# Attention with decay and a mixture of experts on one core: the recorded order of the steps, written anew

## The chip, the cores and the metric

The kernel runs on one core of a Trainium2 chip. The metric is the device time of one execution in microseconds (us). The core's engines are TensorE (PE in the profile, its weight loads PEld), VectorE (DVE), ScalarE (ACT), GpSimd (POOL) and SyncE (SP), which issues nearly all transfers; each works off its own instructions in order and waits for the others at semaphores.

## The reference

Eight batches of eight attention heads (576 positions, 64 columns) with a decay of the scores, then a layer of four experts, each an attention of its own on the 512 columns that the heads give together.

```python
scores = scale * np.matmul(q, k.transpose(0, 1, 3, 2))
cum = np.cumsum(np.log(np.clip(f, 0.0001, 1.0)), axis=-1)
scores = np.where(causal, -1e9, scores + cum[:, :, :, None] - cum[:, :, None, :])
attn = np.exp(scores - np.max(scores, axis=-1, keepdims=True))
attn_out = np.matmul(attn / (np.sum(attn, axis=-1, keepdims=True) + 1e-09), v)
x = attn_out.transpose(0, 2, 1, 3).reshape(B, S, H * D)
for e in range(E):
    q, k, v = x @ wq[e], x @ wk[e], x @ wv[e]
    a = softmax(causal(scale * (q @ k.transpose(0, 2, 1))))
    out += top_two_weight[e] * (a @ v @ wo[e])
```

## The kernel before

The work comes in units of two heads (or two experts): a0_0 to a7_3 are pair 0 to 3 of batch 0 to 7, m0_0 to m7_1 the two pairs of experts of a batch. A name in a profile row is cut to its kind, so ka_a there is the tile ka of some attention unit, ka_m that of a unit of experts; in the listings of the order it keeps its unit, as ka_a1_1.

An attention unit goes through these stages:

- **prep_attn** loads both heads' q and k as xin (L390), and splits them into a high part, rounded by ScalarE's copies (L393, L396), and a low part, the difference of the two, which the subtraction at L406 makes. There are two of it per unit, one per half of the partitions, each 64 partitions by 1152 columns with both inputs in SBUF. VectorE does them, except the first of the units 1 to 3, which GpSimd does. The second subtraction's output ka is what the second half of each scores matmul (L726) reads.
- **max_pass** finds the largest score of each block of rows: matmuls of the high parts into PSUM banks m0 to m3 (L625), VectorE's reductions of them (L631 and L647, inputs in PSUM; L680 and L687 for the last 64 rows) into the tile mxs, a transpose by TensorE (L692), and a copy by ScalarE (L695) that goes back into kq by a transfer. GpSimd first fills a corner of mxs (L621, 64 x 2). The first unit has a form of its own (L585 to L610).
- **scores** computes the scores in banks s0 to s3, two matmuls a piece (L726, L727); ScalarE's exponentials take them into P (L744, L756, L762, L779, L784), GpSimd sets what lies above the diagonal to zero (L713, L747, L786).
- **row_sums**: GpSimd adds up the pieces of P that belong to the same rows in the tile R, for each head one sum of 128x448 (L792), one of 128x320 (L794) and one of 128x192 (L796), and a last one of 64x128 for both (L798). The second and third add to what the one before it wrote in the same half of R. The tile is of 128 partitions, and all their inputs are in SBUF.
- **attend** (L817) multiplies P by the values, **apply_rows** divides by the sums (L855 on TensorE, L870, L873, L875, L884 on VectorE with ScalarE's fill L881 between them, a transfer L890, the product L902).

The experts' units begin with projections (L551 on TensorE, L559 and L564 behind it), and then take the same way.

Every stage of every unit is a Python generator that stops after each step. The table ORDER, two digits in base 64 per step, 5323 steps, says which generator is to go on next, and at the end each engine's instructions are bound to the order in which they were recorded:

```python
for x, y in zip(digits[::2], digits[1::2]):
    i = DIGITS.index(x) * len(DIGITS) + DIGITS.index(y)
    if i not in started:
        started[i] = iter(tasks[i]())
    next(started[i], None)
```

So the table is the order of the work on every engine and in every queue. A second table, SLOTS, says for each kind of tile which buffer the next tile takes, in the order in which they are asked for. The kernel opens with 110 small matmuls that do no work of the reference (L212), spread among the first steps.

Of the kernel before, what the change touches and what calls it, by code (L numbers as in the profile page):

```python
# [27 lines left out]
4w4w4w4w4w4w4w4w4w4w4w4w4w4w4w4w4w4w4w4w4w4w4w4w4w4w4w4w4w4w4w4w4w4w4w4w4w4w4w4w4w4w4w4w4w4w4w4w4w4x4x4x4x000500  # L28
4y4y004x4x4y024y4y4A4y4y4y4y004w4A4w4A4A4w4w4w4A4A4A014A4A4A4A054w4w4w4w4w4w4w050505054w4w4w4w4w4w024w4w4w4w4w4w
4w4w4w4w4w4w4w4w4w0000000000024w024w0202020202020202020c4z4w4w4w4w4w4z074w07074w0207020202020202020202024A4w4w4w  # L30
4w05020202020202050c060c4w4w4w4w07074w4w4A4w020202054w4w0c0c034y0c4y030307070c4w4w4w070703034A4A0703030303070707
030707030303030303074y0h0e4z0707070303030303030303030303034z0707070707074z0e0e0e070e4z0707074z4z0e0e0e0e0e040c0e
0e0e0e0e0e0e0e0j0e0h0h0h0c0h0e0e08080h0e0e03080e0808080h08080808080808080808080o08080t0A0e030j0j0j0j0j0j0j080808
03084w4w0e0e040e0j0j0j0808080o0808030j0j0j0j0j0j0j0j0j0j084w080j0j0j0j0j090e0v0e0o090j0q0t0h0j0o0f0o0f0o0o0j0j0f
0f0f0f0f0f0f030f0f0f0f0f0f0f0f0f0q0q0q0q0q0q0k0q080f0f0q0q0q0f0d080f0f0k0f0f0i080t0f0t030q080k0k0k0k0k0q0q0q0q0q
# [1024 lines left out]
```

## Time and profile before

| | |
|---|---|
| time, median of three runs | 658.17 us (656.69 to 658.58) |
| the profiled execution | 657.54 us |
| its span in the trace | 655.5 us |
| TensorE busy | 633.0 us, 97% |
| VectorE busy | 564.6 us, 86% |
| ScalarE busy | 480.9 us, 73% |
| GpSimd busy | 469.9 us, 72% |
| transfers | 76.91 MB, 117 GB/s |

A row of a timeline has the start of an instruction in us, its duration, its engine and line, the operation, output and inputs, their shapes, how many of them follow each other, and in brackets how long the engine had sat idle before it and what ended that. An instruction that has been taken up by its engine and is held up inside it shows as a long one, without idle time. A windows row has, for a stretch of the span, its length, the busy time of each engine with the number of instructions, the granted clock of TensorE (1.00 is 2.4 GHz, 0.50 is 1.2 GHz), and what the DMA engines did.

### The profile page before, as it was taken

The numbers are of one execution on the slowest core, as the hardware profiler recorded it, in microseconds if no ns is written. First come the engines' busy times: TensorE is split into PE (matmuls) and PEld (weight loads), VectorE is DVE, ScalarE is ACT, GpSimd is POOL, SyncE is SP. The second block draws the span as 40 slices with busy tenths as digits, with TensorE's granted clock in tenths as the row PEclk, the third lists the DMA queues.
The fourth block names the chain that finished last, engine by engine and source line by source line (L and its number), as shares of the span: only waits on it lengthen the run. The fifth ranks groups of instructions, "written<-read, shape, count | busy, mean of one in ns | idle before, by whom it ended". The sixth has DMA issues, their size and how long they took to land.

```text
span 655.5 us, 15384 instructions
## 1 busy us (share of the span) xinstructions
PE 633.0 (97%) x5303; PEld 542.0 (83%) x5303; DVE 564.6 (86%) x1541; ACT 480.9 (73%) x1057; POOL 469.9 (72%) x759
## 2 busy tenths in 40 slices
PE   8897989999999999999999999999999999999997
PEld 6674778888978789779887888977988788979976
DVE  6889798998899998988989899898888998877672
ACT  7896578696777967788677875787758887665644
POOL 9998487879677795769838874877577968814850
PEclk9999899999999999999999999999999999999999
DMA  5553342633454443454544523716344622421236
GB/s 188 156 180 95 91 135 76 180 103 100 95 122 125 135 116 122 123 134 102 148 129 83 142 79 80 196 34 192 95 127 112 197 64 76 110 60 39 61 78 212
DMA packets 33532, 76.91 MB, mean 117 GB/s; under 512 B 4395, under 2 KB 4875, under 8 KB 33455
## 3 DMA queue, kind: packets, MB, share of 16 engines
q1 hardware_dynamic: 33455, 75.94, 42.7%
q8 instruction: 42, 0.69, 0.4%
q14 instruction: 35, 0.29, 0.1%
HBM read 32.86 MB, written 10.35 MB: 66 GB/s over the span
## 4 chain that ended last, share of the span: by engine, by line
PE 76%; DVE 10%; ACT 4%; POOL 4%; DMA 3%; issue 2%; SPq 0%; POOLq 0%; DVEq 0%; ACTq 0%
PE pp_m L551 14%; PE ob_a L817 7%; PE s_a L726 6%; PE po L952 6%; PE s_a L727 6%; PE pv L446 6%; PE m_a L625 6%; PE ob_m L817 4%; PE m_m L625 4%; PE s_m L727 3%; PE s_m L726 3%; DVE ka_a L406 3%; PE oa_a L817 3%; PE sm_a L855 2%; DVE junk_a L631 2%
## 5 line engine op out<-in xcount | busy, mean ns | idle before, releaser
L726 PE MATMUL s_a<-ka_a 128*128 128x320 f32 (+4 forms) x384 | 105.7, 301 | 2.4 <-DVE ka_a L406 1.2
L727 PE MATMUL s_a<-kq 128*128 128x320 f32 (+4 forms) x384 | 103.4, 297 | 0.7 <-DMA kq<-ms_a 0.7
L631 DVE CUSTOM_DVE_ANT_0 junk_a<-m_a,mask 128x192 bf16<-128x192 f32 (+2 forms) x186 | 86.6, 484 | 7.7 <-PE m_a L625 5.2
L625 PE MATMUL m_a<-kq 128*128 128x448 f32 (+3 forms) x372 | 78.1, 305 | 7.2 <-DVE mxs_a L631 6.2
L559 ACT ACTIVATE kq<-pp_m 64x288 fp32r<-64x288 f32 x128 | 51.7, 404 | 34.5 <-PE pp_m L551 32.7
L792 POOL TENSOR_TENSOR R_a<-P_a 128x448 f32<-128x448 f32 x64 | 74.6, 1166 | 0.0
L726 PEld LDWEIGHTS s_a<-ka_a 128*128 128x128 f32 (+1 forms) x384 | 70.3, 183 | 4.9 <-ACT kq L559 1.4
L713 POOL TENSOR_SCALAR_AFFINE_SELECT P_a<-P_a 128x128 f32<-128x128 f32 x128 | 51.2, 408 | 29.5 <-ACT P_a L779 14.2
L747 POOL TENSOR_SCALAR_AFFINE_SELECT P_a<-P_a 128x256 f32<-128x256 f32 x64 | 37.8, 599 | 47.9 <-ACT P_a L744 47.3
L727 PEld LDWEIGHTS s_a<-kq 128*128 128x128 f32 (+1 forms) x384 | 69.7, 183 | 2.2 <-DMA kq<-ms_a 0.9
L564 DVE TENSOR_TENSOR ka_m<-pp_m,kq 64x288 fp32r<-64x288 f32 x128 | 58.2, 455 | 13.1 <-ACT kq L559 9.8
L625 PEld LDWEIGHTS m_a<-kq 128*128 128x128 f32 x372 | 58.5, 182 | 12.8 <-DVE mxs_a L631 7.9
L817 PE MATMUL ob_a<-P_a,va 128*64 128x320 f32 (+1 forms) x512 | 67.6, 406 | 0.0
L794 POOL TENSOR_TENSOR R_a<-R_a,P_a 128x320 f32<-128x320 f32 x64 | 63.8, 997 | 3.3
L406 DVE TENSOR_TENSOR ka_a<-xin_a,ka_a 64x1152 fp32r<-64x1152 f32 x32 | 58.3, 1821 | 0.8
L817 PEld LDWEIGHTS ob_a<-P_a,va 128*64 128x64 f32 x512 | 36.0, 137 | 23.8
L726 PE MATMUL s_m<-ka_m 128*128 128x256 f32 (+3 forms) x192 | 51.4, 294 | 0.0
L727 PE MATMUL s_m<-kq 128*128 128x256 f32 (+3 forms) x192 | 50.8, 293 | 0.0
L631 DVE CUSTOM_DVE_ANT_0 junk_m<-m_m,mask 128x448 bf16<-128x448 f32 (+2 forms) x96 | 44.6, 486 | 6.4 <-PE m_m L625 5.5
L744 ACT ACTIVATE P_a<-s_a 128x512 f32<-128x512 f32 x64 | 36.6, 593 | 13.1 <-PE s_a L727 12.4
L796 POOL TENSOR_TENSOR R_a<-R_a,P_a 128x192 f32<-128x192 f32 x64 | 43.1, 674 | 2.8
L406 DVE TENSOR_TENSOR ka_a<-xin_a,kq 64x1152 fp32r<-64x1152 f32 x29 | 41.5, 1431 | 2.7 <-PE s_m L726 1.9
(206 smaller groups left out, 2096.3 us busy)
## 6 DMA issues: line engine op xcount, KB each, us to landing
xin_a<-in_qk_dram SPq DMA_DIRECT2D x32, 576.0 KB
va<-in_v_dram SPq DMA_DIRECT2D x32, 320.0 KB
bt_a<-rr_a SPq DMA_DIRECT2D x32, 288.0 KB
ka_m<-kq SPq DMA_DIRECT2D x32, 288.0 KB
kq<-ka_a SPq DMA_DIRECT2D x30, 288.0 KB
out_dram<-outb SPq DMA_DIRECT2D x32, 256.0 KB
bt_m<-rr_m SPq DMA_DIRECT2D x16, 288.0 KB
kq<-ex SPq DMA_DIRECT2D x45, 27.0 KB
```

The source lines that it names most:

```text
L406: eng.tensor_tensor(lo, x[at], hi.bitcast(F32), ALU.subtract)
L551: nc.tensor.matmul(pp[:, :HS], w[:, c, es], x[c][:, gs], start=(n == 0), stop=(n == 3 * KC - 1))
L559: nc.scalar.activation(hv[h], src[h], AF.Copy)
L564: nc.vector.tensor_tensor(lo[:, h, gs], src[h], hv[h].bitcast(F32), ALU.subtract)
L625: nc.tensor.matmul(dst, qB[0:K, h, i0 : i0 + dst.shape[0]], kB[0:K, h, j0:j1], start=True, stop=True)
L631: nc.vector.tensor_tensor_reduce(jk[:, :n], src, mask[:, MW - n :], 1.0, init, ALU.add, ALU.max, acc)
L713: return nc.gpsimd.affine_select(pv, pv, [[1, 128]], ALU.is_ge, 0.0, base=0, channel_multiplier=-1)
L726: nc.tensor.matmul(dst, kaf[:, c : c + m], qA[:, h, i0:i1], start=True, stop=False)
L727: nc.tensor.matmul(dst, kqf[0:K, c + h * S : c + h * S + m], qB[0:K, h, i0:i1], start=False, stop=True)
L792: g.tensor_tensor(r[:, h, 128:S], q[:, 320:768], q[:, 768:1216], ALU.add)
L794: g.tensor_tensor(r[:, h, 256:S], r[:, h, 256:S], q[:, 1216:1536], ALU.add)
L817: mm = nc.tensor.matmul(dst[64 * h : 64 * h + 64, c0 : c0 + rhs.shape[-1]], vs[h][0:kp, blk], rhs, start=first, stop=last,)
```

## The change

The tables ORDER and SLOTS are replaced; no other line differs, so line numbers are the same in both kernels, as are the number and the shapes of the instructions of every engine. ScalarE's fill of the reciprocals (L881) stays what it was. Of SLOTS the lines P, wide, banks, mxs, strips and mxt differ.

```diff
 ORDER = """
-4w4w4w4w4w4w4w4w4w4w4w4w4w4w4w4w4w4w4w4w4w4w4w4w4w4w4w4w4w4w4w4w4w4w4w4w4w4w4w4w4w4w4w4w4w4w4w4w4w4x4x4x4x000500
+4w4w4w4w4w4w4w4w4w4y4y4y4y4y4y4y4y4y4w4x4x4x4x000005024w4w4w4w4w4w4w4w4w4w4w4w4w4w4w4w004x004A064w4w4w4w4w4w4w4w
...
 SLOTS = """
-mxs 010101101011001010110101101011010110100101010101
+mxs 010010001011001010110010100011010111010101010101
```

What that moves is shown at three places.

**First, the start, on VectorE.** The first unit's reductions of its first head end with L604; then the kernel before has one of the second unit's reductions (a0_1), and after it the second head of the first unit.

```order
L602 TENSOR_TENSOR mx0_a0_0_282<-m2_a0_0_277,mask_83 64x64
L604 TENSOR_REDUCE mxs_a0_0_182<-mx0_a0_0_282 64x1
L631 ISA junk_a0_1_301,mxs_a0_1_293<-m0_a0_1_296,mask_83 128x192
L631 ISA mxs_a0_1_293 128x1
L595 ISA junk_a0_0_310,mxs_a0_0_182<-m1_a0_0_308,mask_83 128x192
```

```order
L602 TENSOR_TENSOR mx0_a0_0_288<-m2_a0_0_279,mask_83 64x64
L604 TENSOR_REDUCE mxs_a0_0_148<-mx0_a0_0_288 64x1
L595 ISA junk_a0_0_310,mxs_a0_0_148<-m1_a0_0_308,mask_83 128x192
L595 ISA mxs_a0_0_148 128x1
L599 TENSOR_REDUCE mxt_a0_0_217<-m0_a0_0_312 128x1
```

The reduction of a0_1 now stands behind the whole of the second head and behind the subtraction L406 of a0_1.

**Second, the row sums of a0_2 and a0_3 on GpSimd, and VectorE beside them.** GpSimd in the kernel before, from the last zeroing of a0_3 on, and then in the changed one.

```order
L786 AFFINE_SELECT pl0_91<-pl0_91 64x128
L796 TENSOR_TENSOR R_a0_2_725<-R_a0_2_725,P_a0_2_698 128x192
L792 TENSOR_TENSOR R_a0_2_725<-P_a0_2_698 128x448
L792 TENSOR_TENSOR R_a0_3_853<-P_a0_3_775 128x448
L794 TENSOR_TENSOR R_a0_2_725<-R_a0_2_725,P_a0_2_698 128x320
L794 TENSOR_TENSOR R_a0_3_853<-R_a0_3_853,P_a0_3_775 128x320
L796 TENSOR_TENSOR R_a0_2_725<-R_a0_2_725,P_a0_2_698 128x192
L796 TENSOR_TENSOR R_a0_3_853<-R_a0_3_853,P_a0_3_775 128x192
L792 TENSOR_TENSOR R_a0_3_853<-P_a0_3_775 128x448
L621 MEMSET mxs_a1_2_973 64x2
L794 TENSOR_TENSOR R_a0_3_853<-R_a0_3_853,P_a0_3_775 128x320
```

```order
L796 TENSOR_TENSOR R_a0_2_724<-R_a0_2_724,P_a0_2_662 128x192
L786 AFFINE_SELECT pl0_91<-pl0_91 64x128
L792 TENSOR_TENSOR R_a0_3_842<-P_a0_3_772 128x448
L621 MEMSET mxs_a1_1_872 64x2
L794 TENSOR_TENSOR R_a0_3_842<-R_a0_3_842,P_a0_3_772 128x320
L792 TENSOR_TENSOR R_a0_2_724<-P_a0_2_662 128x448
L796 TENSOR_TENSOR R_a0_3_842<-R_a0_3_842,P_a0_3_772 128x192
L792 TENSOR_TENSOR R_a0_3_842<-P_a0_3_772 128x448
L794 TENSOR_TENSOR R_a0_2_724<-R_a0_2_724,P_a0_2_662 128x320
L794 TENSOR_TENSOR R_a0_3_842<-R_a0_3_842,P_a0_3_772 128x320
L796 TENSOR_TENSOR R_a0_2_724<-R_a0_2_724,P_a0_2_662 128x192
L796 TENSOR_TENSOR R_a0_3_842<-R_a0_3_842,P_a0_3_772 128x192
```

Both tables interleave the sums of the two units. In the kernel before a fill of 64 x 2 (L621) stands behind eight sums; in the changed one it stands behind two, ahead of eight.

On VectorE at the same time stands the subtraction L406 of ka_a1_1 that is the second of its unit, first in the kernel before.

```order
L631 ISA junk_a1_1_899,mxs_a1_1_672<-m1_a1_1_897,mask_83,mxt_a1_1_883 128x256
L631 ISA mxs_a1_1_672 128x1
L406 TENSOR_TENSOR ka_a1_1_768<-xin_a1_1_580,ka_a1_1_768 64x1152
L884 STREAM_TRANSPOSE rr_a0_0_920<-zt_a0_0_846 128x576
L631 ISA junk_a1_1_932,mxs_a1_1_672<-m1_a1_1_897,mask_83,mxt_a1_1_883 128x256
L631 ISA mxs_a1_1_672 128x1
L631 ISA junk_a1_1_936,mxs_a1_1_672<-m2_a1_1_934,mask_83 128x448
```

```order
L631 ISA junk_a1_1_900,mxs_a1_1_872<-m1_a1_1_898,mask_83,mxt_a1_1_880 128x256
L631 ISA mxs_a1_1_872 128x1
L884 STREAM_TRANSPOSE rr_a0_0_919<-zt_a0_0_839 128x576
L631 ISA junk_a1_1_921,mxs_a1_1_872<-m1_a1_1_898,mask_83,mxt_a1_1_880 128x256
L631 ISA mxs_a1_1_872 128x1
L406 TENSOR_TENSOR ka_a1_1_754<-xin_a1_1_703,ka_a1_1_754 64x1152
L631 ISA junk_a1_1_930,mxs_a1_1_872<-m2_a1_1_927,mask_83 128x448
```

The subtraction now comes behind the transpose L884 and one more reduction (L631 with its read-out).

**Third, VectorE and GpSimd some 30 us later.** The second subtraction of a1_2 on VectorE, first in the kernel before, then in the changed one; last the row sums of a1_0 and a1_1 that the changed kernel has on GpSimd there.

```order
L631 ISA mxs_a1_3_1142 128x1
L680 TENSOR_TENSOR mx0_a1_3_1284<-m3_a1_3_1278,mask_83 64x128
L687 TENSOR_REDUCE mxs_a1_3_1142<-mx0_a1_3_1284 64x2
L631 ISA junk_a1_3_1289,mxs_a1_3_1142<-m3_a1_3_1287,mask_83 128x320
L631 ISA mxs_a1_3_1142 128x1
L406 TENSOR_TENSOR ka_a1_2_874<-xin_a1_2_582,ka_a1_2_874 64x1152
L564 TENSOR_TENSOR ka_m0_0_1301<-pp_m0_0_1208,kq0_94 64x288 x2
```

```order
L631 ISA mxs_a1_3_1123 128x1
L680 TENSOR_TENSOR mx0_a1_3_1286<-m3_a1_3_1276,mask_83 64x128
L406 TENSOR_TENSOR ka_a1_2_861<-xin_a1_2_721,ka_a1_2_861 64x1152
L564 TENSOR_TENSOR ka_m0_0_1310<-pp_m0_0_1245,kq0_94 64x288 x2
L687 TENSOR_REDUCE mxs_a1_3_1123<-mx0_a1_3_1286 64x2
L564 TENSOR_TENSOR ka_m0_0_1310<-pp_m0_0_1313,kq0_94 64x288 x2
L631 ISA junk_a1_3_1347,mxs_a1_3_1123<-m3_a1_3_1331,mask_83 128x320
```

```order
L786 AFFINE_SELECT pl2_93<-pl2_93 64x128
L792 TENSOR_TENSOR R_a1_0_1060<-P_a1_0_991 128x448
L792 TENSOR_TENSOR R_a1_1_1196<-P_a1_1_1105 128x448
L794 TENSOR_TENSOR R_a1_1_1196<-R_a1_1_1196,P_a1_1_1105 128x320
L796 TENSOR_TENSOR R_a1_1_1196<-R_a1_1_1196,P_a1_1_1105 128x192
L792 TENSOR_TENSOR R_a1_1_1196<-P_a1_1_1105 128x448
L794 TENSOR_TENSOR R_a1_0_1060<-R_a1_0_1060,P_a1_0_991 128x320
L796 TENSOR_TENSOR R_a1_0_1060<-R_a1_0_1060,P_a1_0_991 128x192
```

The subtraction has moved ahead of L687 and of the last reduction of a1_3. On GpSimd each sum L794 of a1_1 and the L796 behind it now directly follow the sum into the same half of R that they add to, and so does the last L796 of a1_0; the kernel before had the sums of a1_0 and a1_1 by turns.

Further on, the first scores matmul of a2_1 is now the 889th matmul on TensorE instead of the 864th, and that of a2_2 the 939th instead of the 981st; the first exponential of a2_2 is row 233 of ScalarE's instead of 236. The transfers are the same in number, and the output's come in the same order.

## Rows read from the trace of the kernel before

**Rows 1.** The page's first part: busy time, share of the span and instructions.

```profile
PE 633.0 (97%) x5303; PEld 542.0 (83%) x5303; DVE 564.6 (86%) x1541; ACT 480.9 (73%) x1057; POOL 469.9 (72%) x759
```

**Rows 2.** Windows: start and end, length, busy per engine, PEclk, DMA share, GB/s.

```profile
0.00:25.00 25.00, 20.82 (x145) 16.60 (x145) 18.02 (x45) 19.52 (x25) 23.54 (x33) 1.00 0.59 184
25.00:50.00 25.00, 22.82 (x175) 18.75 (x174) 21.92 (x71) 22.32 (x43) 24.21 (x44) 1.00 0.55 167
50.00:68.00 18.00, 12.27 (x104) 8.34 (x103) 17.70 (x37) 9.56 (x18) 13.66 (x21) 0.92 0.41 107
68.00:86.00 18.00, 17.30 (x124) 14.31 (x124) 14.60 (x34) 13.16 (x31) 9.65 (x19) 0.89 0.30 74
86.00:110.00 24.00, 21.68 (x171) 18.97 (x170) 22.68 (x52) 17.79 (x38) 19.54 (x28) 1.00 0.43 126
...
135.00:635.00 500.00, 496.33 (x4299) 429.82 (x4299) 440.38 (x1233) 369.63 (x843) 359.69 (x587) 1.00 0.42 109
```

**Rows 3.** Timeline of VectorE, 50 to 65 us.

```profile
51.04 1.35 DVE L406 TENSOR_TENSOR ka_a<-xin_a,kq 64x1152 fp32r<-64x1152 f32 x1
...
55.74 7.57 DVE L406 TENSOR_TENSOR ka_a<-xin_a,ka_a 64x1152 fp32r<-64x1152 f32 x1
63.33 0.78 DVE L884 STREAM_TRANSPOSE rr_a<-zt_a 128x576 f32<-128x576 f32 x1
64.04 0.44 DVE L631 CUSTOM_DVE_ANT_0 junk_a<-m_a,mask,mxt_a 128x256 bf16<-128x256 f32 x1
```

**Rows 4.** Timeline of GpSimd, 51 to 64.3 us.

```profile
51.29 1.26 POOL L713 TENSOR_SCALAR_AFFINE_SELECT P_a<-P_a 128x128 f32<-128x128 f32 x1 [0.32 <-ACT P_a L762]
...
53.63 0.28 POOL L713 TENSOR_SCALAR_AFFINE_SELECT P_a<-P_a 128x128 f32<-128x128 f32 x1
...
55.22 0.29 POOL L786 TENSOR_SCALAR_AFFINE_SELECT pl<-pl 64x128 f32<-64x128 f32 x1
55.48 0.58 POOL L796 TENSOR_TENSOR R_a<-R_a,P_a 128x192 f32<-128x192 f32 x1
56.03 2.23 POOL L792 TENSOR_TENSOR R_a<-P_a 128x448 f32<-128x448 f32 x2
58.23 1.68 POOL L794 TENSOR_TENSOR R_a<-R_a,P_a 128x320 f32<-128x320 f32 x2
...
62.03 0.09 POOL L621 MEMSET mxs_a<- 64x2 f32 x1
62.16 1.86 POOL L794 TENSOR_TENSOR R_a<-R_a,P_a 128x320 f32<-128x320 f32 x1
```

**Rows 5.** Timeline of TensorE, 60 to 68 us.

```profile
64.55 1.32 PE L625 MATMUL m_a<-kq 128*128 128x192 f32 x4 [4.49 <-DVE mxs_a L631]
67.09 0.38 PE L692 MATMUL mp_a<-ident,mxs_a 128*10 128x128 f32 x1 [1.22 <-DVE mxs_a L631]
```

**Rows 6.** Timeline of VectorE, 90 to 97 us.

```profile
90.91 4.17 DVE L406 TENSOR_TENSOR ka_a<-xin_a,ka_a 64x1152 fp32r<-64x1152 f32 x1
95.12 1.88 DVE L564 TENSOR_TENSOR ka_m<-pp_m,kq 64x288 fp32r<-64x288 f32 x4
```

**Rows 7.** Timeline of GpSimd, 88 to 96 us.

```profile
88.29 0.29 POOL L786 TENSOR_SCALAR_AFFINE_SELECT pl<-pl 64x128 f32<-64x128 f32 x1
...
92.71 1.16 POOL L792 TENSOR_TENSOR R_a<-P_a 128x448 f32<-128x448 f32 x1
```

**Rows 8.** Timeline of TensorE, 94 to 96 us.

```profile
95.23 0.33 PE L726 MATMUL s_a<-ka_a 128*128 128x192 f32 x1 [1.19 <-DVE ka_a L406]
```

**Rows 9.** Timeline of VectorE, 16 to 18 us.

```profile
17.01 0.36 DVE L631 CUSTOM_DVE_ANT_0 junk_a<-m_a,mask 128x192 bf16<-128x192 f32 x1
```

**Rows 10.** Timeline of TensorE, 22 to 23 us.

```profile
22.66 0.36 PE L727 MATMUL s_a<-kq 128*128 128x192 f32 x1 [0.72 <-DMA kq<-ms_a]
```

**Rows 11.** Timeline of ScalarE, 154 to 165 us.

```profile
156.54 0.27 ACT L695 ACTIVATE ms_a<-mp_a 10x128 fp32r<-10x128 f32 x1 [2.70 <-PE mp_a L692]
...
163.29 0.60 ACT L744 ACTIVATE P_a<-s_a 128x512 f32<-128x512 f32 x1 [0.98 <-PE s_a L727]
```

More of the change, by code (lines that the diff above doesn't have):

```diff
@@ new lines @@
+4w4w4w4w4w4w4w4w4w4w4w4w4w4w4w4w4w4w4w4w4w4w4w4w4w4w4w4w4w4w4w4w4w024w4w4A4w4w4w4w4w4w4A4A4A4A4A4A4A4A4A4w4w4A4A
+4w4w4w4w4w4A4w4x0000000000020205020202054w4w020202024w4w024z0502024w0c4z4w05054w4w4w054w0202020202020c4y4y0e0202
+02020202020202024w4w4w4w4w4w4w4w4w4w014w4w02074w07070c0205070707070207070303030c070c4A0c0c0303030h07030303030303
+030707074y0307030303030707030707070707070707030303030303030e0e0e0e07070e0e4z4z4z4z4z4z0e0e0e0c03030707070e0d040e
+0h0j4w0e0e0e0e0e0e0h0h0h0e050c0h0e0e0e0e0e0e0803080808080o0308040808080e0808030e0h08080e03080j0j0j0j0j0e0j0j0j0j
@@ new lines @@
+0j084w080808080808080808084w0j0o0j0e0j0j08080j0j0j0j0j0j0j0j0j0o0j0j08030i080h0f0f0f0f0f0f0f0f0f0f0f0C0f0908090t
+0t030o0f0j0j0f080o0f0o0o0A0f0f080q0q0q0q0q0q4w0j0j0q0f0f0f0f0f0t0q080q0t0t0q0q0k0k0q0k0q0q0q0f0q0k040q0k0k080q0k
+0f0k0f0q0k0q0f0q0q0k0q0q0q0k0f0f0A0q0f0k0k0k0k0a0a0k0k0k0F0k0k0k0k0k0a0k0k0A0k0q0f0q0k0k0t0v0v0k0v0v0v0A0v0f0a0k
+0q0a0A0v0q0a0v0v0v0v0g0v0a0v0v0k0o0g0v0t0v4A0t0v0v0v0v0v0v0v0v0F0f0a0l0C0C0C0C0g090k0f0v0r0k0r0r0r0r0r0r0p0l0b0C
+0C0C0r0C0v0C0C0r0r0f0v0v0r0v0v0b0C0a0k0B0C0C0C0C0C0C0C0l0C0r0r0r0r0r0r0r0r0r0r0r0r0r0C0r0C0w0F0w0r0C0r0N0b0C0m0w
@@ new lines @@
+0M0w0r0m0F0m0w0m0m0H0C0C0m0m0b0b0F0m0b0b0w0w0w0m0w0w0w0w0s0s0w0b0A0H0H0b0r0w0w0H0H0n0r0Y0w0H0w0w0C0H0w0w0w0w0n0s
+0H4A0b0b0H0n0n0n0n0C0R0M0H0n0R0R0n4A0N0N0w0R0H0M0H0n0H0H0H0H0H4A0H0H0H0H0w0w0w0w0r0H0N0M0A0N0C0w0w0N0C0w0w0u0N0R
+0N0N0N0N0M0A0N0N0N0N0H0r0H0N0N0N0N0N0N0N0H0N0N0N0N0N0N0N0N0N0r0N4A0D0N0D0N0D0D0D0r0D0D0D0O0O0O0O0N0D0D0D0D0w0N0N
+0O0R0O0O0O0H0D0O0D0D0D0O0M0M0M0O0D0D0D0D0D0D0D0H0H0O0O0H0H0D0w0M0F0M0M0O0M0F0F0w4A0Y0D0O0O0O0O0O0O0O0O0x4y0y0I0x
+0D0R0D0D0O0y0y0y0y0Y0I0I0I0D0Y0I0I0I0I0I0Y0O0N0I0I0D0O0I0I0I0I0I0I0I0I0I0I0I0I0R0n0n0y0Y0x0O0y0O0O0O0O0Z0R0R0R0R
@@ new lines @@
+0R0I0R0R0R0I0R0R0+0R0R0R0R0I0I0I0I0I0I0I0I0+0+0D0R0R0R0R0R0R0R0R0+0+0M0+0R0R0+0+0R0P0P0+0D0M0R0I0S0S0S0S0S0S0S0P
+0P0y0P0D0S0S4y0R0S0S0y0M0+0P0P0P0P0P0P0P0M0M0P0P0+0S0S0S0S0S0S0S0S0+0M0M0P0S0+0S0+0+0+0M0M0M0+0M0S0S0S0S0M0M0M0S
+0D0+0P0+11110R0M0M0R0P0P0M0P0P0P0P0P0P0P0P0P0P0P0P0G0M0z0+0K0S0K0+0S0z0K0K110K0+0+0+0R0z0+0E0Y0K0K0Y180J181a0S0J
+4y0+0E0E0+0S0T0T110T0T0T0T130T0T11110T0T0T0T1d0+11131313130T0T0T0T0T0T0T0z0T0K0K0T1313131313130T180T0M0+0+0M0T0Q
+0T0T0T0T0T0T0M0M0M130L0M13130Q0-130L0-0-0-130Q1313130-130-13130-13130-0-0-0-0-0z0-130-0-0M0M0-0-0L0-0-0-0L0z1818
@@ new lines @@
+0P0-0z4A134A1a1a1a0z0M1a1a1a1a1a0P1a1a0-130-0U130L0z0-0-0-0-0U1a1d1a1a1a1a1f13131a1a1a1a1a1a1a1a1d1d0M1a1k1k1a0M
+11190P0J0M0T0M0M0M0T0T10100U18181d181a0M0T1a0z10140P1a14141414141414141414141414141414140L0L1414141f140V0M0V0M0M
+1a1f1f0L1f1b1f1b1b0V1b1b1f1l141b1b1b1b141l1f1f0-1f140V0-0-1b0L14141414141f1b1b4A1b1l1l1l1d1b1f1b1f1l0L1l0L1l1l1l
+1b1b1b1f1f1f1l1l0V1p1f1p1b1l1b1l1l0-0V4A4A1b1l1l0-1f1f1d0V1e1l1b1f1l1f1f1p1p1p1p1p1l1p1p1p1f1k1k1k1k1k1k1f1f1l1l
+1l1l1l1l1l1l1l1l1l1l0-0-1m1f1d1l1l1p1p141b1b1b1b1b121m1f1l1l1f1f1f1k1p1p1k1k1k4y1m1m1m1m1m1m1m1m1m1414141p1p1p1p
@@ L123 @@
+4q4q4q4q4q4q4q4q4q4n4n3b4n3L4n4q4q4q4p4n4n4n4n4n4n4n4n4n4n4p4h4h4h4h4n4n4h484q4q3L4n483X4k4k4k4k4k4k4k4k4k4k4k4k
+4k4k4k4k4k4n4n4n4q4q4r4r4r4r4r4r4r4r4r4r4r4r4r4r4r4r4r4r4r4r4r4r4r4r4r4r4k4k4k4r4k4k484k4k3L4h4h4h4h4h4k4r4r3L3L
+3L3L4r4r4r4r3L3L3L3L4k4k4n4k4k4k4k4k4k4k4k4k4k4i3L4g4r4o4i4k4n4t4k4t4k4t4t4s4k4g4t4t4i4g4o4i4i4i4t4t4s4s3L4i4i4i
+4i4i3L4t4t3L3L3L3L4o3L4u4u4u4u4u4j4j4j4j4j4j4j4u4u4j4j4j4j4j4j4j4u4u4u4j4j4v4u4v4v4v4v4v4v4v4v4v4v4v4v4v4v4v4v4v
 4v4v4v
```

169 lines of the change are left out of this document (70 added, 99 removed).

## The prediction

> **What bounds the kernel now.** I read the page's busy times first: TensorE is busy 633.0 us of a span of 655.5 [rows 1], so all that any order can win from its idle time is 22.5 us. The windows say where that lies [rows 2]. From 135 to 635 us TensorE is busy 496.33 of 500 us, and nothing that another engine does sooner shortens that. In the first 110 us it is idle 4.18, 2.18, 5.73, 0.70 and 2.32 us, 15.1 together. In 50 to 68 and 86 to 110 us VectorE is the busiest, 17.70 of 18 and 22.68 of 24. And the granted clock is 0.92 and 0.89 in the two stretches from 50 to 86 us: one minus the clock, times 18 us, gives 1.44 and 1.98 us, so 3.4 us of full-speed time were lost.
>
> The timelines show why. VectorE's subtraction L406 is taken up at 55.74 us and lasts 7.57 us, where the one at 51.04 lasts 1.35 [rows 3]: it was held up for 6.2 us. GpSimd meanwhile does row sums back to back, with a first gap only at the fill L621 at 62.03 us [rows 4]; 63.31 minus 1.35 is 61.96, so L406 got in just there. The sum that GpSimd starts next takes 1.86 us, where two of its kind took 1.68 together. The reverse is seen at 51.04: L406 starts first, and GpSimd's L713 lasts 1.26 us instead of 0.28 [rows 3, 4]. So L406 and GpSimd's work exclude each other. TensorE pays: it waits 4.49 us for a reduction behind L406, and another 1.22 soon after [rows 5], and then works at the lower clock of the windows above (1.2 GHz) for twice 3.4, some 6.8 us. The same happens, smaller, at 90.91 us: L406 lasts 4.17 us, 2.8 too long, while GpSimd's sums run to 93.87 us, and TensorE waits 1.19 us for it [rows 6 to 8].
>
> **The change, part by part.** Nothing is added or removed; all is place.
>
> *The start.* VectorE's reduction of a0_1 (0.36 us, the next start 0.43 us behind it) stood between the two heads of a0_0 [rows 9]. On the second head hangs the transfer for which TensorE waits 0.72 us at 22.66 [rows 10]. So the second head, its transfer and the scores behind it come 0.43 us sooner: I take −0.4. The ends are 0 (ScalarE's exponentials, which come next, were the limit after all) and −1.2, all of the wait and the 0.43 with it. GpSimd's fills move too, but behind them VectorE waits for TensorE's first maxima, which don't move; that costs nothing unless a fill comes over 1 us late.
>
> *The first jam.* In the kernel before the run that held L406 up began at 55.48 and ended at the fill. In the changed one the fill comes early: L796, L786, one sum L792, the fill, and then eight sums without a fill and with no sum directly behind the one whose result it adds to. From the start at 55.22, with 0.29, 0.58 and half of 2.23 us [rows 4], the fill falls at 57.2, and with the 0.4 us of the start at 56.8. L406 now has the transpose (0.78) and a reduction (0.44 with its read-out inside the next step) ahead of it [rows 3]: 55.74 + 1.2 − 0.4 gives 56.5 to 56.6, if neither waits. So the subtraction arrives within a few tenths of the fill. If it is there by the fill it is free at once; if not, it waits for three L794, two L792 and three L796: 3 × 0.84 + 2.23 + 3 × 0.58 = 6.5 us [rows 4], against 6.2 now. I take the second. VectorE is the engine without slack here, so whatever comes late on it adds to the 56.6 (the transpose waits for ScalarE's fill of the reciprocals, which lies two stages before it, and the transposes L870 now stand ahead of the unit's first subtraction), while GpSimd, busy 13.66 of 18 us, is where the table says. The term is 0: 0.3 us more of waiting, against one reduction that the maxima have behind them before the jam. The ends are −9.1 (both TensorE waits, 5.7, and the clock's 3.4) and +0.6 (the longer run and a fill that no longer splits it).
>
> That L406 waits through a whole run, and not just for one sum, is the trace's. The Trainium skill (SBUF — State Buffer, "Who interferes with whom") says that a VectorE instruction with two inputs in SBUF and a GpSimd instruction that reads SBUF exclude each other, and that the one first issued holds the shared ports for the whole instruction. The trace agrees with the exclusion; but a hold that ended with an instruction would have let L406 in after at most one L792, and 6.2 us is more than five of them. By the rule as it is written the changed kernel's L406 would wait 1.1 us at most, and the term would be −5.7; I go by the row.
>
> *The second jam.* L406 of a1_2 moves ahead of L687 and of a reduction, so it comes some 0.8 us sooner, and GpSimd's sums beside it are no longer by turns: L794 stands directly behind the L792 into which it adds, and L796 behind that. In the kernel before GpSimd left its gap at exactly such a place, after the L792 that ended at 93.87 [rows 7]. So L406 should get in after one sum at the longest and the rest of another, about 0.8 us on average, where it waited 2.8. That is 2.0 us of VectorE, which has no slack in this stage [rows 2]: I take −2.0. The ends are −1.2, TensorE's own wait for it [rows 8], and −2.3, all of TensorE's idle time of the stage; and 0 if the sums run on nonetheless.
>
> *The rest.* From 110 us on the units keep their places within some 5 us of work. TensorE is busy anyway, other waits of two-input VectorE instructions cost it nothing there. I take 0, with ±2.
>
> The sum on the profiled execution: 657.54 − 0.43 − 2.0 = 655.1. That execution lies 0.63 us under the median of the runs shown, 658.17, so the forecast is **655.7 us**. About 0.3%, 2.0 us, is what a measurement of this kernel can tell from no change: faster means below 656.2, slower above 660.1.
>
> **The rivals.**
>
> *Both jams go* (0.23). L406 of a1_1 is there by the fill; it needs to be only 0.3 us sooner than I fear, and the shorter wait at the start helps. Then TensorE's two waits of 5.7 us go as well, 655.7 − 5.7 = 650.0; with the lower clock gone too it would be 646.6, with a third of the 5.7 given back at the next wait for VectorE 652. Against it stands the order: two instructions more ahead of it.
>
> *The hold ends with the instruction* (0.03), the rule above. As a mechanism of this kernel: no L406 waits longer than 1.1 us wherever it stands, the first jam cannot come again, and the time is 650.0 as well. The 7.57 us in the trace speak against it.
>
> *TensorE waits for ScalarE at a2_1 and a2_2* (0.20), on the other side. The scores of a2_2 stand 42 matmuls sooner. By 633.0 us over 5303 records that is 5.0 us, over 4311 instructions 6.2; I take 5.5. ScalarE's exponential of them stands only three instructions sooner, some 1.4 us, and those of a2_1 come later than they did. The banks that the scores fill are freed by these exponentials. In the kernel before ScalarE had time to spare here: it waited 2.70 and 0.98 us for TensorE at 156.54 and 163.29 [rows 11]. If this is used up, TensorE waits 5.5 − 1.4 = 4.1 us, and more if its clock falls as in the first jam. With a second jam that shrinks to half this gives 657.5 + 4.1 − 1 + 0.6 = 661. It decides once the two units' exponentials and the copies among them take longer than the 50 matmuls that now lie between the units' first scores, 5.9 to 7.4 us by the same two counts. Against it: seven exponentials of 0.6 us are 4.2.
>
> *Nothing to be told* (0.18): the second jam is won and another L406 is caught in another run of sums, or the 2.4 us are waited for later, before 110 us, by the same VectorE: 658.
>
> **How the numbers follow.** The forecast has 0.36, with a range of its own from 653.5 to 657.5. Of its 0.36 some 0.22 lie below 656.2. With 0.23, 0.03 and a little of the last case that makes faster 0.50. Same takes the other 0.14 of the forecast, most of the last case and a little of the ScalarE one: 0.28. Slower is 0.19 of the ScalarE case and 0.03 of the last: 0.22. The range reaches from 648.5, which leaves out the third of the first rival in which the clock's gain comes whole, to 661.5, which leaves out the upper half of the ScalarE case.
>
> **What would show it.** Right: an L406 of over 6 us near 57 to 65 us with TensorE waiting for a reduction behind it and a granted clock under 1 after it; no L406 above 2.5 us between 85 and 95 us; TensorE full from 135 us on. Wrong: no L406 above 3 us in the first 110 us and a time near 650; or a wait of TensorE of over 2 us for an exponential's bank between 145 and 170 us and a time above 660.

## The result, and the profile after

The changed kernel takes 647.38 us (median of four runs, 646.38 to 651.12) where the kernel before, in the same job, takes 658.12; the ratio on record, which goes by all runs and not by the two medians, is 0.9851 with an interval of 0.9807 to 0.9895. The prediction was 655.7 with a range of 648.5 to 661.5: the direction was right, the time lies below the range.

The profiled execution took 646.38 us, with a span of 644.5 against 655.5. The page's first part, to hold against [rows 1]:

```profile
PE 628.1 (97%) x5303; PEld 538.3 (84%) x5303; DVE 553.1 (86%) x1541; ACT 483.3 (75%) x1057; POOL 475.8 (74%) x759
```

TensorE's idle time fell from 22.5 to 16.4 us, by 6.1, and its busy time by 4.9, though it does the same matmuls: the mean granted clock rose from 0.995 to 0.999, so the full-speed time lost to the lower level fell from 0.005 x 655.5 = 3.3 us to 0.6. This execution is the quickest of the four; the other three have mean clocks of 0.992, 1.000 and 0.995, so not each one loses so little. The windows, in the columns of [rows 2]:

```profile
0.00:25.00 25.00, 19.78 (x146) 16.57 (x147) 17.87 (x44) 19.70 (x26) 23.53 (x33) 1.00 0.61 186
25.00:50.00 25.00, 20.09 (x156) 15.61 (x155) 23.48 (x62) 19.59 (x36) 23.25 (x41) 1.00 0.51 158
50.00:68.00 18.00, 16.76 (x135) 12.32 (x136) 16.64 (x49) 15.15 (x30) 16.99 (x27) 1.00 0.44 120
68.00:86.00 18.00, 18.00 (x149) 15.48 (x148) 16.87 (x43) 13.71 (x35) 14.68 (x21) 1.00 0.58 156
86.00:110.00 24.00, 24.00 (x200) 22.08 (x199) 20.80 (x55) 19.82 (x45) 21.66 (x33) 1.00 0.29 67
...
135.00:624.00 489.00, 487.74 (x4230) 422.46 (x4228) 427.46 (x1204) 365.48 (x829) 358.30 (x577) 1.00 0.42 110
```

TensorE's idle time by stretch is now 5.22, 4.91, 1.24, 0 and 0 us where it was 4.18, 2.18, 5.73, 0.70 and 2.32 [rows 2], and the clock is 1.00 in both stretches from 50 to 86 us. So most of the gain lies where the first and the second jam were, and 25 to 50 us has become worse. From 135 to 624 us TensorE is idle 1.3 of 489 us, where it was idle 3.7 of 500, so another 2.4 us were won there: two waits of 1.0 and 1.1 us for a reduction (L692 for L631, between 200 and 250 and between 450 and 500 us) are gone. The wait for ScalarE that one rival saw at a2_1 and a2_2 did not come.

VectorE's timeline shows the L406 rows that the prediction spoke of, for [rows 3] and [rows 6]:

```profile
41.79 4.85 DVE L406 TENSOR_TENSOR ka_a<-xin_a,kq 64x1152 fp32r<-64x1152 f32 x1
46.67 1.35 DVE L406 TENSOR_TENSOR ka_a<-xin_a,ka_a 64x1152 fp32r<-64x1152 f32 x1
...
59.83 2.16 DVE L406 TENSOR_TENSOR ka_a<-xin_a,ka_a 64x1152 fp32r<-64x1152 f32 x1
...
84.73 1.73 DVE L406 TENSOR_TENSOR ka_a<-xin_a,ka_a 64x1152 fp32r<-64x1152 f32 x1
```

The subtraction that lasted 7.57 us lasts 2.16, at 59.83, and the one of a1_2 1.73 instead of 4.17. A new one is held up: at 41.79 us one lasts 4.85. GpSimd beside the first two, for [rows 4]:

```profile
39.55 0.29 POOL L786 TENSOR_SCALAR_AFFINE_SELECT pl<-pl 64x128 f32<-64x128 f32 x1
39.81 1.14 POOL L792 TENSOR_TENSOR R_a<-P_a 128x448 f32<-128x448 f32 x1
...
43.01 0.09 POOL L621 MEMSET mxs_a<- 64x2 f32 x1
43.07 0.58 POOL L796 TENSOR_TENSOR R_a<-R_a,P_a 128x192 f32<-128x192 f32 x1
43.62 0.45 POOL L798 TENSOR_TENSOR R_a<-R_a,pl 64x128 f32<-64x128 f32 x1
...
44.30 1.13 POOL L792 TENSOR_TENSOR R_a<-P_a 128x448 f32<-128x448 f32 x1
46.46 0.34 POOL L713 TENSOR_SCALAR_AFFINE_SELECT P_a<-P_a 128x128 f32<-128x128 f32 x1 [1.03 <-ACT P_a L762]
...
58.66 0.09 POOL L621 MEMSET mxs_a<- 64x2 f32 x1
58.80 0.88 POOL L794 TENSOR_TENSOR R_a<-R_a,P_a 128x320 f32<-128x320 f32 x1
59.63 1.14 POOL L792 TENSOR_TENSOR R_a<-P_a 128x448 f32<-128x448 f32 x1
60.73 1.71 POOL L796 TENSOR_TENSOR R_a<-R_a,P_a 128x192 f32<-128x192 f32 x1
```

At 59.83 L406 comes 1.2 us **after** the fill (58.66), in the midst of the eight sums. By the prediction's picture it should have been kept out to the end of the run: 6.5 us from 58.80 on, of which 5.5 were left. It began at 61.99 - 1.35 = 60.64, about with the end of the L792 that was running, and the next sum, L796, took 1.71 us instead of 0.6. At 41.79 it is the other way round: a fill passed at 43.01 and L406 did not get in; it began at 46.64 - 1.35 = 45.29, when GpSimd's L792 of 44.30 ended and GpSimd stood idle. Eight instructions went by. Two lines of what TensorE waited for in the first 115 us (us in all, times, longest):

```profile
PE m_a L625 <- DVE mxs_a L631: 2.3, 3, 1.1
PE s_a L726 <- DVE mxt_a L647: 1.2, 1, 1.2
```

The wait of 4.49 us [rows 5] is gone; the 1.2 us for L647 are those behind the hold at 41.79.

So the prediction's picture of what keeps VectorE out was wrong. The three longest holds of the two kernels stand in runs of GpSimd that have an L786 (64 partitions) in them, with no pause between it and the hold: at 55.22 us [rows 4], 88.29 [rows 7] and now 39.55. The eight sums at 58.80 have none among them; the last one lies ahead of the fill, and behind the fill GpSimd paused for 0.05 us. Three theories went into the experiments: **A**, an instruction on part of the partitions makes GpSimd keep VectorE out from there until it next pauses; **B**, the prediction's, any run without a wait for its own result does; **C**, the rule weighed in the prediction, a hold never outlasts one instruction.

### The profile page after: what moved, and what is told of

It is laid out like the page before. It is cut to its first block, busy times and chain, and to the rows that moved or that the text cites. A ratio compares the mean times of both kernels' runs of the same rounds, so it can differ in the third digit from the quotient of the medians.

```text
span 644.5 us, 15370 instructions
## 1 busy us (share of the span) xinstructions
PE 628.1 (97%) x5303; PEld 538.3 (84%) x5303; DVE 553.1 (86%) x1541; ACT 483.3 (75%) x1057; POOL 475.8 (74%) x759
## 4 chain that ended last, share of the span: by engine, by line
PE 83%; POOL 7%; DVE 4%; ACT 2%; issue 1%; DMA 1%; SPq 0%; POOLq 0%; DVEq 0%; ACTq 0%
PE pp_m L551 14%; PE ob_a L817 8%; PE po L952 8%; PE pv L446 7%; PE s_a L726 7%; PE s_a L727 7%; PE m_a L625 6%; PE ob_m L817 5%; PE m_m L625 4%; PE s_m L726 4%; PE s_m L727 4%; PE oa_a L817 3%; PE sm_a L855 3%; PE oa_m L817 2%; DVE ka_a L406 2%
## 5 line engine op out<-in xcount | busy, mean ns | idle before, releaser
L631 DVE CUSTOM_DVE_ANT_0 junk_a<-m_a,mask 128x448 bf16<-128x448 f32 (+2 forms) x186 | 87.0, 485 | 11.9 <-PE m_a L625 9.9
L625 PE MATMUL m_a<-kq 128*128 128x448 f32 (+2 forms) x372 | 79.8, 303 | 3.5 <-DVE mxs_a L631 2.3
L792 POOL TENSOR_TENSOR R_a<-P_a 128x448 f32<-128x448 f32 x64 | 75.1, 1174 | 0.0
L713 POOL TENSOR_SCALAR_AFFINE_SELECT P_a<-P_a 128x128 f32<-128x128 f32 x128 | 54.1, 432 | 27.3 <-ACT P_a L779 12.9
L794 POOL TENSOR_TENSOR R_a<-R_a,P_a 128x320 f32<-128x320 f32 x64 | 64.3, 1006 | 3.5
L747 POOL TENSOR_SCALAR_AFFINE_SELECT P_a<-P_a 128x256 f32<-128x256 f32 x64 | 34.7, 546 | 34.4 <-ACT P_a L744 33.9
L726 PE MATMUL s_m<-ka_m 128*128 128x192 f32 (+2 forms) x192 | 51.4, 294 | 0.4 <-DMA ka_m<-kq 0.4
L727 PE MATMUL s_m<-kq 128*128 128x192 f32 (+2 forms) x192 | 51.3, 293 | 0.0
L631 DVE CUSTOM_DVE_ANT_0 junk_m<-m_m,mask 128x192 bf16<-128x192 f32 (+2 forms) x96 | 44.8, 486 | 5.1 <-PE m_m L625 3.8
L406 DVE TENSOR_TENSOR ka_a<-xin_a,ka_a 64x1152 fp32r<-64x1152 f32 x32 | 47.5, 1484 | 0.7
L406 DVE TENSOR_TENSOR ka_a<-xin_a,kq 64x1152 fp32r<-64x1152 f32 x29 | 46.5, 1603 | 1.5 <-PE s_a L726 0.8
L796 POOL TENSOR_TENSOR R_a<-R_a,P_a 128x192 f32<-128x192 f32 x64 | 45.2, 708 | 2.7
```

Source lines behind the costliest of these rows:

```text
L406: eng.tensor_tensor(lo, x[at], hi.bitcast(F32), ALU.subtract)
L625: nc.tensor.matmul(dst, qB[0:K, h, i0 : i0 + dst.shape[0]], kB[0:K, h, j0:j1], start=True, stop=True)
L631: nc.vector.tensor_tensor_reduce(jk[:, :n], src, mask[:, MW - n :], 1.0, init, ALU.add, ALU.max, acc)
L713: return nc.gpsimd.affine_select(pv, pv, [[1, 128]], ALU.is_ge, 0.0, base=0, channel_multiplier=-1)
L726: nc.tensor.matmul(dst, kaf[:, c : c + m], qA[:, h, i0:i1], start=True, stop=False)
L727: nc.tensor.matmul(dst, kqf[0:K, c + h * S : c + h * S + m], qB[0:K, h, i0:i1], start=False, stop=True)
```

## The experiments

### The same orders, with L786 and L798 on all partitions

The upper half of the tile p4 is set to zero once and stays zero under the select, so both instructions may take 128 partitions. Nothing else changes; the order is that of the kernel before in one run, that of the changed kernel in the other.

```diff
-            p4[:64], p4[:64], [[0, 2], [1, 64]], ALU.is_ge, 0.0, base=0, channel_multiplier=-1
+            p4, p4, [[0, 2], [1, 64]], ALU.is_ge, 0.0, base=0, channel_multiplier=-1
...
-        u["summed"] = g.tensor_tensor(r[0:64, :, 512:S], r[0:64, :, 512:S], p4[:64], ALU.add)
+        u["summed"] = g.tensor_tensor(r[:, :, 512:S], r[:, :, 512:S], p4, ALU.add)
```

Expected with the order before:

> Theory A (64 partitions): behind an instruction of GpSimd that reads SBUF on 64 partitions only (L786, L798), GpSimd keeps VectorE's two-input instructions out until it pauses; behind full ones only until the running instruction ends. Then here, where L786 and L798 take all 128 partitions (the upper half of the tile is zero and stays zero), no L406, L902 or L929 is held for more than 1.2 us, L406 at 55.7 us lasts 1.4 to 2.5 us instead of 7.57, the one at 90.9 about 1.5 to 2.5 instead of 4.17, TensorE's waits of 4.49 and 1.22 us go, and the time is 646 to 652 us. Theory B (unbroken run, as in the prediction): the hold lasts until GpSimd has to wait for its own last result or does a fill, whatever the partitions: L406 stays at 7.57 and 4.17 us and the time at 658 +- 1. Theory C (single instruction): a hold never outlasts one instruction and the long L406 has another cause, which this edit does not touch: 658 +- 1.

Measured: 642.35 us (641.58 to 643.06, four runs), ratio 0.977 (0.9755 to 0.9785). VectorE and GpSimd in this run, where the kernel before had its first jam:

```profile
55.65 1.55 DVE L406 TENSOR_TENSOR ka_a<-xin_a,ka_a 64x1152 fp32r<-64x1152 f32 x1
57.23 0.78 DVE L884 STREAM_TRANSPOSE rr_a<-zt_a 128x576 f32<-128x576 f32 x1
...
91.97 1.35 DVE L406 TENSOR_TENSOR ka_a<-xin_a,kq 64x1152 fp32r<-64x1152 f32 x1
93.33 1.35 DVE L406 TENSOR_TENSOR ka_a<-xin_a,ka_a 64x1152 fp32r<-64x1152 f32 x1
```

```profile
55.13 0.29 POOL L786 TENSOR_SCALAR_AFFINE_SELECT pl<-pl 128x128 f32<-128x128 f32 x1
55.40 0.59 POOL L796 TENSOR_TENSOR R_a<-R_a,P_a 128x192 f32<-128x192 f32 x1
55.95 3.36 POOL L792 TENSOR_TENSOR R_a<-P_a 128x448 f32<-128x448 f32 x2
59.27 1.68 POOL L794 TENSOR_TENSOR R_a<-R_a,P_a 128x320 f32<-128x320 f32 x2
```

The run of sums is the same, and L406 comes at the same point of it (55.65, before 55.74). It now lasts 1.55 us: it got in behind the L796 of 55.40, and the two L792 together took 3.36 us instead of 2.23, since one of them waited for it. No L406 of the kernel lasts over 2.2 us:

```profile
L406 DVE TENSOR_TENSOR ka_a<-xin_a,ka_a x32: 1343/1356/2025, 11.1 to 538.7; 64x1152 fp32r<-64x1152 f32 x32
L406 DVE TENSOR_TENSOR ka_a<-xin_a,kq x29: 1345/1355/2193, 9.8 to 536.9; 64x1152 fp32r<-64x1152 f32 x29
```

The profiled execution's clock is 1.00 throughout. B and C expected no change, A expected this one. The gain, 15 us, is even larger than the 6 to 12 expected, and this kernel, the **old order with two instructions widened, has the lowest median of the study and beats both kernels of the change**.

Expected with the changed order:

> The same edit in the changed kernel. Theory A: its L406 of 4.85 us at 41.8 us (held for 3.5 us behind an L786) falls to 1.4 to 2.5 us, the longest hold of any two-input instruction is 1.2 us, TensorE's idle time between 25 and 50 us falls from 4.9 us by 1 to 3, and the time is 644 to 646.5 us. Theories B and C: L406 stays at 4.85 us, time 647.4 +- 1.

Measured: 645.38 us (643.9 to 648.5, four runs), ratio 0.9823 (0.9793 to 0.9852). The L406 of 4.85 us lasts 1.77 (at 43.23), no two-input instruction is held for over 1 us, and TensorE is idle 2.1 us between 25 and 50 us instead of 4.9. Theory A again. But with the holds gone in both, the new order is not the better one: in this pair its interval lies above that of the old order. A part of that is the clock: it is 0.96 and 0.98 in the first two stretches of 25 us here, some 1.5 us of full-speed time, and 1.00 in those of the old order's run. Most of what the new order wins, it wins by where the holds fall.

### A narrow instruction put into the run of eight

The changed kernel gets one instruction more, on a tile of its own that nothing else reads, behind the first of the eight sums: a select on 64, on 128 or on 96 partitions, or a fill of 64 x 128. (In all four that tile is also filled once at the opening.)

```diff
-            g.tensor_tensor(r[:, h, 256:S], r[:, h, 256:S], q[:, 1216:1536], ALU.add)
+            g.tensor_tensor(r[:, h, 256:S], r[:, h, 256:S], q[:, 1216:1536], ALU.add); nm == "_a0_3" and h == 0 and g.affine_select(spare[:64], spare[:64], [[0, 2], [1, 64]], ALU.is_ge, 0.0, base=0, channel_multiplier=-1)
```

> The changed kernel with one more instruction on GpSimd, a select of 64 x 128 on a tile of its own, right behind the first of the eight sums (L794 of a0_3). Theory A: L406 of a1_1 (2.16 us at 59.8 us now) is then held to about the end of the run, 5 to 7 us in all, TensorE waits 3 to 5 us for a reduction behind it, and the time is 652 to 657 us. Theory B: the run is as long as it was, L406 gets in as before or is held as before by luck of its arrival, time 647.4 + 0.3, at most +1. Theory C: L406 is held for at most 1.2 us, 647.4 + 0.3.

Measured: 653.12 us (651.51 to 653.92, four runs), ratio 0.9927 (0.9906 to 0.9948). The jam of the kernel before is back, at a place where the changed kernel had none:

```profile
61.16 6.83 DVE L406 TENSOR_TENSOR ka_a<-xin_a,ka_a 64x1152 fp32r<-64x1152 f32 x1
```

```profile
60.05 0.10 POOL L621 MEMSET mxs_a<- 64x2 f32 x1
60.19 0.88 POOL L794 TENSOR_TENSOR R_a<-R_a,P_a 128x320 f32<-128x320 f32 x1
61.02 0.29 POOL L794 TENSOR_SCALAR_AFFINE_SELECT spare<-spare 64x128 f32<-64x128 f32 x1
61.28 1.13 POOL L792 TENSOR_TENSOR R_a<-P_a 128x448 f32<-128x448 f32 x1
...
65.65 1.13 POOL L796 TENSOR_TENSOR R_a<-R_a,P_a 128x192 f32<-128x192 f32 x2
```

```profile
PE m_a L625 <- DVE mxs_a L631: 5.5, 2, 4.4
```

The select of 64 x 128 takes 0.29 us. L406 came during it, 0.14 us behind its start, and lasts 6.83 us; it began at 67.99 - 1.35 = 66.64, with the end of the run at 66.77. TensorE waits 4.4 us at once, and the clock of the profiled execution is 0.88 from 50 to 68 us and 0.85 from 68 to 86.

> The control of the run before: the same extra instruction in the same place, of 128 x 128. All theories: L406 of a1_1 is held for at most 1.2 us, time 647.4 + 0.3, between 646.5 and 648.5. If this one jams as well, it is the extra instruction and not its partitions.

Measured: 646.11 us (645.56 to 647.74, four runs), ratio 0.9832 (0.9814 to 0.9849), a little under the range expected:

```profile
60.22 1.35 DVE L406 TENSOR_TENSOR ka_a<-xin_a,ka_a 64x1152 fp32r<-64x1152 f32 x1
```

```profile
60.01 0.30 POOL L794 TENSOR_SCALAR_AFFINE_SELECT spare<-spare 128x128 f32<-128x128 f32 x1
60.27 2.31 POOL L792 TENSOR_TENSOR R_a<-P_a 128x448 f32<-128x448 f32 x1
```

L406 came 0.21 us behind the start of the select (0.14 in the run before), and was not held; the L792 behind it took 2.31 us instead of 1.13, since now GpSimd waited. Same instruction, same place, same arrival, all partitions: no jam, and 7.0 us less than with 64. This settles A against B: the run goes on without a pause in both, for 5.7 us from the select of 64 partitions on and for longer here.

> The changed kernel with the extra select in the run of eight on 96 partitions instead of 64 or 128. If any instruction that leaves out some partitions starts a hold, L406 at 60 us lasts over 6 us and the time is 652 to 654; if it takes half of them, L406 lasts under 2.5 us and the time is 646 to 647.5.

Measured: 652.56 us (652.52 to 655.1, three runs), ratio 0.9929 (0.9897 to 0.996). The time is that of 64 partitions (with a second fall of the clock in it, 0.93 from 110 to 135 us), but the held instruction is another. In this execution L406 met only a short hold at 42 us (2.13 us long), came by at 57.59, before the run, and it was the product L902 that was caught, so that the L406 of over 6 us that was expected is not there:

```profile
57.59 1.36 DVE L406 TENSOR_TENSOR ka_a<-xin_a,ka_a 64x1152 fp32r<-64x1152 f32 x1
...
62.34 4.44 DVE L902 TENSOR_TENSOR ot_a<-bt_a,ot_a 128x576 f32<-128x576 f32 x1
```

```profile
67.91 1.76 PE L625 MATMUL m_a<-kq 128*128 128x256 f32 x6 [4.21 <-DVE mxs_a L631]
```

It was held for 3.7 us behind the select of 96 partitions (59.63 us), past six ends of GpSimd's instructions, and TensorE waited 4.21 us. So it need not be half of the partitions; one instruction that leaves out a quarter of them does it.

This execution also shows what theory A gets wrong. L902 got in behind the second L747 of GpSimd's run, at 66.1 us, and GpSimd had not paused. And at 42.13 us L406 came 2.24 us behind the same L786 that holds it in four other executions of this order:

```profile
42.13 2.13 DVE L406 TENSOR_TENSOR ka_a<-xin_a,kq 64x1152 fp32r<-64x1152 f32 x1
```

```profile
39.89 0.29 POOL L786 TENSOR_SCALAR_AFFINE_SELECT pl<-pl 64x128 f32<-64x128 f32 x1
...
42.64 1.88 POOL L747 TENSOR_SCALAR_AFFINE_SELECT P_a<-P_a 128x256 f32<-128x256 f32 x2
```

It got in behind the first L747, after 0.8 us, and the second one waited for it (1.88 us for the two instead of 0.76). In the changed kernel, and in the runs with the select of 64, of 128 and with the fill, L406 came 2.24 or 2.25 us behind that L786 too, GpSimd's order was the same, and it was held for 3.5 us. What decides between the two is not known. So behind a narrow instruction VectorE may be kept out past many ends, but neither always nor always until the next pause.

> The changed kernel with a fill of 64 x 128 (which reads nothing) in the place of the extra select in the run of eight. If what starts a hold is any instruction on part of the partitions, L406 at 60 us lasts over 6 us and the time is 652 to 654; if it has to read its input from SBUF, L406 lasts under 2.5 us and the time is 646 to 647.5.

Measured: 654.43 us (653.79 to 654.56, three runs), ratio 0.9935 (0.9911 to 0.996), a little over the range expected:

```profile
62.23 6.67 DVE L406 TENSOR_TENSOR ka_a<-xin_a,ka_a 64x1152 fp32r<-64x1152 f32 x1
```

```profile
62.02 0.20 POOL L794 MEMSET spare<- 64x128 f32 x1
```

L406 is held for 5.3 us behind the fill. So it need not read either. The fills of 64 x 2 (0.09 us) that stand in all these kernels, the two widened ones too, went with no hold over 1.1 us; whether that is their size was not tried.

### One jam at a time

The widened select for one unit only: L786 of a0_3 in the kernel before (the first jam), L786 of a1_1 there (the second), L786 of a0_1 in the changed kernel (its own hold at 41.8 us).

```diff
-        made[5] = g.affine_select(
-            p4[:64], p4[:64], [[0, 2], [1, 64]], ALU.is_ge, 0.0, base=0, channel_multiplier=-1
+        wide_ = 128 if nm in ("_a0_3",) else 64; made[5] = g.affine_select(
+            p4[:wide_], p4[:wide_], [[0, 2], [1, 64]], ALU.is_ge, 0.0, base=0, channel_multiplier=-1
```

> The kernel before with one single select on 128 partitions: L786 of a0_3, the one ahead of the run that held L406 for 6.2 us. Theory A: L406 at 55.7 us lasts under 2.5 us, TensorE's waits of 4.49 and 1.22 us go and its clock stays at 1.00 after them; the second jam at 90.9 us may stay, it is not touched. If the price of the first jam is waits and clock together, 5.7 + 3.4, the time falls by 8 to 9.1 us, to about 648.5; if it is VectorE's 6.2 us alone, to 651; if half is waited for later, to 653. Theory B: nothing changes, 657.5.

Measured: 649.0 us (648.79 to 649.49, four runs) beside 657.83, ratio 0.9863 (0.9837 to 0.9888). One instruction of 0.29 us, widened, is worth 8.8 us. The second jam stays as it was, only earlier:

```profile
55.74 1.56 DVE L406 TENSOR_TENSOR ka_a<-xin_a,ka_a 64x1152 fp32r<-64x1152 f32 x1
...
81.94 4.18 DVE L406 TENSOR_TENSOR ka_a<-xin_a,ka_a 64x1152 fp32r<-64x1152 f32 x1
```

The price is that of the waits and the clock together (5.7 + 3.4 = 9.1), not VectorE's 6.2 alone: the clock is 1.00 from 50 to 110 us in this run.

> The kernel before with the select L786 of a1_1 alone on 128 partitions, the one ahead of the run that held L406 for 2.8 us at 90.9 us. Theory A: L406 lasts under 2.5 us there. The prediction's term was VectorE's 2.0 us; the other end was TensorE's own wait, 1.2 us: time 655.2 by the first, 656 by the second, from 657.3. The first jam stays.

Measured: 655.31 us (654.08 to 656.82, twelve runs), ratio 0.9958 (0.9943 to 0.9973), so 2.5 us by the medians and 1.8 to 3.7 by the interval. L406 at 91.04 us lasts 1.40, the first jam is there with 7.57. VectorE's 2.0 us of the prediction fits, TensorE's own 1.2 is outside the interval.

> The changed kernel with the select L786 of a0_1 alone on 128 partitions, the one ahead of its own hold of 3.5 us at 41.8 us. Theory A: L406 lasts under 2.5 us there, TensorE is idle 2 to 3 us between 25 and 50 us instead of 4.9, and the time is that of the run with all selects and last sums on 128 partitions within 1 us, 644.5 to 646.5: the hold at 41.8 is what the changed order still pays. If the time stays at 646.5 to 647.5, that hold is off the path that sets the end.

Measured: 643.69 us (641.81 to 644.89, four runs), ratio 0.9774 (0.974 to 0.9807), against 0.9851 (0.9807 to 0.9895) for the changed kernel, each against the kernel before in its own job. L406 lasts 1.76 us at 42.24, and TensorE is idle 2.2 us between 25 and 50 us. The hold at 41.8 costs the changed kernel 3.7 us by the medians, though the two intervals meet at 0.9807, so the size is rough. Without it, the new order can't be told from the old one without its holds (642.35). The time lies under the 644.5 to 646.5 expected, and 1.7 us under the run of this order with all selects and sums widened.

## Why the prediction was wrong

**What bounds the kernel: right in the main.** Most of the gain came from the first 110 us, out of the two jams and the lower clock behind the first. The 0 put down for the rest was too small a gain: behind 135 us TensorE's idle time fell by 2.4 us, from 3.7 to 1.3.

**The start: right in kind, somewhat smaller, not timed by itself.** The second head's reductions end 0.28 us sooner (L604 at 19.68 instead of 19.96) and the scores that waited for the transfer start at 22.41 instead of 22.66 [rows 10]. The step took 0.43. A fill on GpSimd does come late there (VectorE waits 1.38 us for L576, and the first L595 starts at 13.87 instead of 12.52), but the L595 behind that one starts at 14.79 instead of 15.15, 0.36 us sooner than it did, so the late fill cost nothing, as the prediction had it.

**The first jam: wrong, and this is the step that failed.** It said: "if it is there by the fill it is free at once; if not, it waits for three L794, two L792 and three L796", 6.5 us, and so put the term at 0. L406 was not there by the fill, and waited 0.81 us. The jam's price in the kernel before is 8.8 us, as the first single widening shows, so the term was about -8.8. Behind it lay a picture drawn from two cases, that GpSimd holds VectorE off as long as it need not wait for its own result. Both cases had an L786 just ahead of the sums. The run of eight in the changed kernel had none, and held L406 for no longer than the instruction that was running; with a select of 64 partitions put into it the jam is back, with one of 128 it is not. The prediction had both L786 in its rows with their 64 partitions, yet never asked what the runs that held had in common and what those that didn't hold lacked: in the trace of before, 55 of VectorE's two-input subtractions and products (L406, L902, L929) came while GpSimd was in a run with no narrow select, sum or subtraction ahead of them in it, and none of them was held for over 1.1 us or past the end of the instruction behind the running one. That count could have been made before.

**The times of arrival: also wrong.** Fill and L406 were put at 56.8 and 56.6 us and came at 58.66 and 59.83. The hold at 41.79, which the prediction did not see, lies between. It stands behind an L786 as the others do.

**The rule of the Trainium skill** (SBUF — State Buffer, "Who interferes with whom"), that the one first issued holds the shared ports for the whole instruction: in runs of full instructions the traces agree. At 59.83 L406 waited 0.81 us, and in the two kernels with all selects and last sums widened no hold is over 1.1 us. Behind a narrow instruction they often don't: 6.2 us, 5.5, 5.3, 3.5. The prediction set the rule aside because of the 6.2 us; it should have kept it for the runs in which nothing spoke against it, and it would have given -5.7 there.

**The second jam: right, a little too small.** The term was -2.0; the single widening measured 2.5 (1.8 to 3.7). In the changed kernel L406 of a1_2 lasts 1.73 us, and it got in where the prediction said, at the pause between an L792 and the L794 that adds to it:

```profile
82.98 2.26 POOL L792 TENSOR_TENSOR R_a<-P_a 128x448 f32<-128x448 f32 x2
85.32 1.88 POOL L794 TENSOR_TENSOR R_a<-R_a,P_a 128x320 f32<-128x320 f32 x1
```

**The clock: seen, priced and then left out.** The rival "both jams go" had 646.6 us for the waits and the clock together, which is within 0.8 us of what was measured, but its middle was put at 650.0 without the clock, and the range cut at 648.5. The single widening shows that the clock's part came nearly whole: -8.8 of 9.1. That 646.6 lies so near is in part luck: what this rival needed, L406 there by the fill, did not happen, and the sum below has two terms that it lacks.

**The sum, as it was:** -8.8 and -2.5 for the two jams of before, +3.7 for the new hold, make -7.6; the change measured -10.7. The other 3.1 us lie in the rest of the order, and the 2.4 us of TensorE's idle time that went behind 135 us would be most of them. The widened old order, too, won more (15 us) than the two jams (11.3). What removed those later waits in the changed order was not tried.

## What to carry to other kernels

An instruction of GpSimd that leaves out some partitions is not cheap because it is small: in a run of back-to-back work beside it, VectorE's two-input instructions may be kept out past many of its instructions, so fill the other partitions up, where that costs nothing, before an order is searched that steps round it. Here two lines gave 15 us in the old order, where the two large jams were; in the new one, 2.0 us by the medians, with intervals that overlap. Where a trace shows a rare long stall, compare the cases that stall with the many like them that don't before a mechanism is drawn from the stalls alone. And where a stall lets TensorE's clock fall, its price is the wait and the slow stretch after it.

## What the runs showed of the hardware

- Over the eleven profiles of this study 841 of VectorE's L406, L902 and L929 came while GpSimd was in a run (no pause of 20 ns or more) with no select, sum or subtraction on 64 partitions ahead of them in it. 839 got in by the end of the instruction behind the running one at the latest, none held for over 1.1 us; the other two are the ones caught behind the added select of 96 partitions and behind the added fill, for 3.7 and 5.3 us.
- Of 255 that came with such an instruction ahead of them in the run, 27 were kept out past two ends or more, up to 6.2 us. Of these 27 and the two above, 23 got in where GpSimd next paused; five short holds (0.4 us) ended behind a fill of 64 x 2, and the 3.7 us behind 96 partitions ended between two instructions. The others were not held past two ends: many such runs pause soon after (L794 directly behind its own L792 pauses for 0.08 us), and at least 14 got in behind a later instruction of a run that went on without a pause. So every long hold of this study has a narrow instruction ahead of it, but not every narrow instruction makes one. Why it does it, no run here can show.
- The added select took 0.29 to 0.30 us on GpSimd on 64, on 96 and on 128 partitions alike. With 64 or 96 the program takes 653.12 and 652.56 us, with 128 it takes 646.11, which can't be told from the 647.38 without it.
